# Two parts of packed k in PSUM banks of their own, and idle matmuls between a prologue's TensorE work

## The chip, the cores and the metric

The kernel runs on one core of a Trainium2 chip. The metric is the device time of one execution in microseconds (us), lower being better. An execution is called fast unless it is more than 1.5% above the fastest of its kernel. A profile adds the span (first to last instruction of the core), some 1.7 us less than the device time, and the granted clock of TensorE as a mean over the span.

The profile shows five engines side by side: TensorE (PE, busy for 226.4 us of the 237.5 us span of the kernel before, and PEld for its weight loads, 127.5 us), VectorE (DVE, 115.4 us), ScalarE (ACT, 92.6 us), GpSimd (POOL, 48.4 us) and SyncE (SP), which issues all transfers here but one of 4 KB.

## The reference

A block-wise linear attention with decay, and after it a bilinear feed-forward layer (FFN). Cut to what matters:

```python
batch, n_heads, seq, head_dim = (4, 8, 768, 64)
for b in range(nb):                       # blocks of one sequence
    intra = einsum('bhic,bhjc->bhij', qb, kb) * Dmask
    intra = einsum('bhij,bhjd->bhid', intra, vb)
    inter = einsum('bhid,bhde->bhie', qb * lam_pow, kv_state)
    out[:, :, sl] = intra + inter
    kv_state = lam_block * kv_state + einsum('bhsd,bhse->bhde', kb * rev_pow, vb)
# x: 3072 tokens x 512
return ((x @ w_a) * (x @ w_b)) @ w_out    # 512 -> 1536 -> 512
```

The inputs are float32; the kernel computes in bf16 with float32 sums.

## The kernel before

Tokens are handled as 24 units of 128. The first four units are "packed": their q and k come in as large transfers, two halves of heads each, are scaled on VectorE, transposed on TensorE into PSUM and copied out by ScalarE (`unpack`). Then come score products, a mask on VectorE, state products, outputs into `xT`, and from there the FFN, which fills the rest of the kernel. The work on later units is slipped in between FFN matmuls.

```python
def ps_bank(name, shape, dt, hold=False, ffn=False):   # seven banks in turn
    i = bank["next"]
    ...
    return ps_pool.tile(shape, dt, name=name, tag=f"ps{i}")

def warm(n, cols=128):                                 # idle matmuls on zeros
    for _ in range(n):
        nc.tensor.matmul(idle_ps[:, :cols], lhsT=idle_sb[:, :128], rhs=idle_sb[:, :cols], ...)

def load4(w, i, parts):                                # one half of packed q or k
    ...
    tps = ps_bank("t" + w, [128, 2, PACK, 128], BF16)
    for j in range(2):
        hs = slice(4 * i + 2 * j, 4 * i + 2 * j + 2)
        nc.vector.tensor_mul(...)                      # scale by the decay
        for r in range(PACK):
            nc.tensor.transpose(tps[:, j, r, :], xs4[w][:, r, ...], ident)
        if parts == 2:
            unpack(i, tps, slice(j, j + 1), w)         # ScalarE copies this part out
    if parts == 1:
        unpack(i, tps, slice(0, 2), w)

warm(13, 512)
...
for w, parts in (("q", 1), ("k", 2)):
    for i in range(2):
        load4(w, i, parts)
        if w == "q":
            warm(4)
...
scores4(0)
natural_k((0, 1, 2), (0, 1))
natural_k((0, 1, 2), (2, 3))
scores4(1)
sts = [ps_bank("kv0", ...), ps_bank("kv1", ...), kv_bank()]
for hh in range(2):                                    # state products, by halves
    for u, ps in enumerate(sts):
        for w in range(u + 1):
            kv_mms(ps, w, range(2 * hh, 2 * hh + 2), w == 0)
        if hh:
            kv_copy(u, ps, ("act", "act", "dve")[u])
# ... intra, inter and evac_o of the four units; then the FFN
```

For k, the two parts of a half are copied out one by one, but both lie in one bank: in the profile of before, the transposes of the second part wait for the copy of the first (TensorE idle for 0.67 us in each half, until ScalarE's copy ends).

## Time and profile before

| | device time, us |
|---|---|
| median of 3 runs | 238.28 (237.89 to 238.35) |
| the profiled run | 239.18 (span 237.5, mean clock 0.983) |

The first two lines here are from the page of the profiled run: its span, and the granted clock over 40 equal slices of it, in tenths (9 is 90% or more). The third is from TensorE's timeline: start, length, what, and in brackets how long TensorE was idle before and what ended it.

```profile
span 237.5 us, 4496 instructions
PEclk9959999999999999999999999999999999999998
21.12 1.89 PE L413 MATMUL a_ps<-xT,wa_sb 128*128 128x512 bf16 x7 [0.45 <-ACT xT L352]
```

The slice with a 5 lies in the prologue, where the clock is at half from 10.84 to 17.66 us; in the last slice it falls at 236.09 us, after TensorE's work. The FFN starts at 21.12 us, the moment ScalarE has made its last copy into xT. From there TensorE is nearly solid (busy for 210.37 of the 216.38 us left).

### The profile page before, as it was taken

Reading aid. Unit: us, or ns where it says so; the run is one execution under the profiler, and the core shown is the slowest. Engines: PE = TensorE matmul, PEld = TensorE weight load, DVE = VectorE, ACT = ScalarE, POOL = GpSimd, SP = SyncE. Lnnn points to the kernel's source line nnn. Section 1 sums busy time; section 2 is a strip of 40 time slices with the busy share of each in tenths; the row PEclk is TensorE's granted clock in tenths of the full one; section 3 lists DMA queues with packets and bytes.
Section 4 is the critical chain, followed back from the end, with each engine's and each line's share of the span. In section 5 each row is a group of like instructions: output and inputs, shape, how many; then the busy total and the mean of one; then the engine's idle time right before and its main releaser. Section 6 shows DMA issues by size and latency. Waiting matters only on the chain.

```text
span 237.5 us, 4496 instructions
## 1 busy us (share of the span) xinstructions
PE 226.4 (95%) x1738; PEld 127.5 (54%) x1761; DVE 115.4 (49%) x205; ACT 92.6 (39%) x174; POOL 48.4 (20%) x63
## 2 busy tenths in 40 slices
PE   7599999999999999999999999999999999999993
PEld 2375444458788754454544454544454544444493
DVE  0875756735757646675145575135564214332050
ACT  3548565036554542332143242242341233431161
POOL 6050001234336443203305503003300000000000
PEclk9959999999999999999999999999999999999998
DMA  4999999999979999997929969613120220000311
GB/s 157 297 292 350 348 368 278 284 215 280 228 176 222 191 222 230 222 180 123 212 100 213 185 59 236 150 70 82 27 47 0 88 88 4 0 0 24 111 44 48
DMA packets 94278, 38.32 MB, mean 161 GB/s; under 512 B 81200, under 2 KB 89776, under 8 KB 94256
## 3 DMA queue, kind: packets, MB, share of 16 engines
q1 hardware_dynamic: 94112, 38.02, 70.0%
q8 instruction: 14, 0.23, 0.4%
q14 instruction: 8, 0.07, 0.1%
q10 hardware_dynamic: 144, 0.00, 0.0%
HBM read 28.32 MB, written 6.29 MB: 146 GB/s over the span
## 4 chain that ended last, share of the span: by engine, by line
PE 89%; ACT 3%; DMA 3%; issue 1%; DVE 1%; SPq 0%; DVEq 0%; ACTq 0%
PE a_ps L413 27%; PE b_ps L413 26%; PE op L434 26%; DMA q<-in_q_dram 3%; PE o_ps L345 2%; PE kq L308 2%; PE kvd L359 2%; PE o_ps L335 1%; PE tps L294 1%; ACT scratch L517 1%; ACT xT L352 1%; PE kq L542 1%; ACT o_sb L429 1%; PE tn L526 1%; DVE scratch L503 1%
## 5 line engine op out<-in xcount | busy, mean ns | idle before, releaser
L425 DVE TENSOR_TENSOR ab<-a_sb,b_ps 128x512 bf16<-128x512 bf16 (+2 forms) x96 | 52.6, 553 | 82.7 <-PE b_ps L413 60.2
L413 PE MATMUL a_ps<-xT,wa_sb 128*128 128x512 bf16 (+2 forms) x378 | 76.6, 325 | 1.4 <-ACT xT L352 0.6
L413 PE MATMUL b_ps<-xT,wb_sb 128*128 128x512 bf16 (+2 forms) x379 | 76.7, 325 | 0.2
L420 ACT CAST a_sb<-a_ps 128x512 bf16<-128x512 f32 (+2 forms) x96 | 45.5, 480 | 66.1 <-PE a_ps L413 64.5
L434 PE MATMUL op<-wo_sb,ab 128*128 128x512 bf16 (+2 forms) x300 | 64.3, 362 | 0.9 <-issue 0.5
L413 PEld LDWEIGHTS <-wb_sb 128*128 128x128 bf16 x384 | 34.5, 98 | 28.8 <-issue 0.2
L413 PEld LDWEIGHTS <-wa_sb 128*128 128x128 bf16 x384 | 33.6, 98 | 28.0 <-issue 1.3
L434 PEld LDWEIGHTS <-ab 128*128 128x128 bf16 x312 | 28.7, 98 | 30.1
L320 DVE TENSOR_TENSOR m<-kq,lotri 128x512 bf16<-128x512 f32 x48 | 29.9, 683 | 22.5 <-PE kq L308 20.5
L256 POOL TENSOR_TENSOR qk<-kf,lp_k 128x512 bf16<-128x512 f32 x17 | 17.9, 1051 | 79.9 <-issue 33.5
L429 ACT COPY o_sb<-op 128x512 f32<-128x512 f32 (+2 forms) x26 | 14.2, 553 | 37.2 <-PE op L434 36.7
L261 POOL TENSOR_TENSOR qk<-qf,lp_q 128x512 bf16<-128x512 f32 x20 | 22.0, 1099 | 23.9 <-DMA qf<-in_q_dram 23.9
L352 ACT CAST xT<-o_ps 128x512 bf16<-128x512 f32 x23 | 12.4, 589 | 16.4 <-PE o_ps L345 16.4
L381 DVE TENSOR_TENSOR st<-kvd,bdiag 128x512 bf16<-128x512 f32 x18 | 12.3, 685 | 3.8 <-PE kvd L359 3.8
L296 ACT COPY qkT<-tps 128x1024 bf16<-128x1024 bf16 x7 | 7.1, 1012 | 11.2 <-PE tps L294 11.2
L270 DVE CAST vb<-vf 128x512 bf16<-128x512 f32 x17 | 9.2, 541 | 0.0
L345 PE MATMUL o_ps<-m,vb 128*64 128x128 bf16 x192 | 7.8, 222 | 0.0
L270 POOL CAST vb<-vf 128x512 bf16<-128x512 f32 x7 | 4.4, 630 | 15.6 <-DMA vf<-in_v_dram 15.6
L335 PEld LDWEIGHTS <-st 128*128 128x128 bf16 x80 | 5.4, 98 | 2.8
L308 PE MATMUL kq<-qkT 64*128 64x128 bf16 x160 | 6.6, 218 | 0.0
L345 PEld LDWEIGHTS <-vb 128*64 128x64 bf16 x192 | 5.7, 109 | 1.4
L359 PEld LDWEIGHTS <-qk 128*128 128x128 bf16 x64 | 4.9, 98 | 2.9
(52 smaller groups left out, 87.5 us busy)
## 6 DMA issues: line engine op xcount, KB each, us to landing
vf<-in_v_dram SPq DMA_DIRECT2D x24, 256.0 KB, 5.2
out_dram<-o_sb SPq DMA_DIRECT2D x23, 256.0 KB, 2.3
qf<-in_q_dram SPq DMA_DIRECT2D x20, 256.0 KB, 4.5
kf<-in_k_dram SPq DMA_DIRECT2D x20, 256.0 KB, 4.8
wst<-in_moe_w_a_dram SPq DMA_DIRECT2D x6, 512.0 KB, 9.0
wst<-in_moe_w_b_dram SPq DMA_DIRECT2D x6, 512.0 KB, 8.9
wst<-in_moe_w_out_dram SPq DMA_DIRECT2D x6, 512.0 KB, 8.5
q<-in_q_dram SPq DMA_DIRECT2D x2, 512.0 KB, 5.5
```

Source lines behind the costliest of these rows:

```text
L256: eng_of(eng).tensor_mul(qk[:, 1], raw.pop((u, "k")), lp_k[:, u % NB].to_broadcast([128, H, D]))
L261: eng_of(eng).tensor_mul(U[u]["qk"][:, 0], raw.pop((u, "q")), lp_q[:, u % NB].to_broadcast([128, H, D]))
L270: eng_of(eng).tensor_copy(vb, vf)
L320: nc.vector.tensor_mul(m, kq[i], lotri_bc)
L345: nc.tensor.matmul(d["o"][p, hp, :], lhsT=d["vb"][:, 2 * hp + i, :], rhs=d["m"](i, hp), start=(first and hp == 0), stop=True, skip_group_c ...
L352: nc.scalar.copy(xT[:, :, col:col + BLK], o_ps)
L381: nc.vector.tensor_mul(st[:].rearrange("p hp i d -> p hp (i d)"), ps[:].rearrange("p hp i d -> p hp (i d)"), bdiag_bc)
L413: nc.tensor.matmul(ps[:, :gt], lhsT=w_sb[:, s, f * 128:(f + 1) * 128], rhs=xT[:, s, :gt], start=(s == 0), stop=(s == KS - 1))
L420: nc.scalar.copy(a_sb[:, :gt], ps[:, :gt])
L425: nc.vector.tensor_mul(ab[:, f, :gt], a_sb[:, :gt], ps[:, :gt])
L429: nc.scalar.copy(o_sb[:, lo:hi], op[:, lo:hi])
L434: nc.tensor.matmul(op[:, lo:hi], lhsT=ab[:, f, t * 128:(t + 1) * 128], rhs=wo_sb[:, f, lo:hi], start=(f == 0), stop=(f == FC - 1))
```

## The change

The intent: let the second part of k be transposed without waiting for the first one's copy, and put short idle matmuls where TensorE has gaps so that its clock isn't lowered in the prologue.

```diff
@@ def load4(w, i, parts):
-        tps = ps_bank("t" + w, [128, 2, PACK, 128], BF16)
         for j in range(2):
+            if j == 0 or parts == 2:
+                tps = ps_bank("t" + w, [128, 2, PACK, 128], BF16)
...
             if parts == 2:
                 unpack(i, tps, slice(j, j + 1), w)
+                if i == 0 or j == 0:
+                    warm(3)
@@
     scores4(0)
     natural_k((0, 1, 2), (0, 1))
+    warm(2)
     natural_k((0, 1, 2), (2, 3))
+    warm(2)
     scores4(1)
+    warm(4)
```

## The prediction

> **What bounds the kernel now.** I read the page first, then the chain of waits that ended last, then the timeline of TensorE, of its weight loads and of the other engines over the first 22 us, then stretches of that time with the granted clock. The page says where most of the time is:
>
> ```profile
> PE 226.4 (95%) x1738; PEld 127.5 (54%) x1761; DVE 115.4 (49%) x205; ACT 92.6 (39%) x174; POOL 48.4 (20%) x63
> PE 89%; ACT 3%; DMA 3%; issue 1%; DVE 1%; SPq 0%; DVEq 0%; ACTq 0%
> ```
>
> TensorE is the chain for 89% of the span. The stretches 22 to 60, 60 to 120 and 120 to 237.5 us show it busy for 37.29, 59.36 and 112.89 us. So from the first FFN matmul, at 21.12 us, the rest is a nearly solid stream of about 216 us that the change doesn't touch. All that can move is the time at which that first matmul starts, and that is set by the prologue: the four packed units at 6 to 21 us. There the chain goes from engine to engine:
>
> ```profile
> 9.09 1.57 ACT scratch L517 x2
> 10.70 0.50 PE tk L508 x4
> 11.22 1.15 ACT scratch L517 x2
> 12.41 0.59 PE tk L508 x4
> 13.00 0.97 PE kq L542 x16
> 13.96 1.39 PE tn L526 x12
> 15.36 0.97 PE kq L542 x16
> 16.32 0.75 PE kv L359 x6
> ```
>
> (start, length, what). Two things in it are aimed at. The first is that TensorE's transposes of k (L508) twice wait for ACT's copy (L517) of the previous part, which lies in the same PSUM bank. The weight-load lines show how long the transposes could have been running already:
>
> ```profile
> 10.23 0.10 PEld L508 LDWEIGHTS <-scratch 128*128 128x128 bf16 x1 [0.38 <-DVE scratch L503]
> 10.70 1.04 PE L508 MATMUL tk<-ident,scratch 128*128 128x128 bf16 x8 [0.67 <-ACT scratch L517]
> 11.73 0.10 PEld L508 LDWEIGHTS <-scratch 128*128 128x128 bf16 x1 [0.26 <-DVE scratch L503]
> 12.41 0.59 PE L508 MATMUL tk<-ident,scratch 128*128 128x128 bf16 x4 [0.67 <-ACT scratch L517]
> ```
>
> The weights are in at 10.23 and 11.73 us, the moment VectorE is done, but the matmuls start at 10.70 and 12.41: 0.47 and 0.68 us late. The second is the clock:
>
> ```profile
> 0.60:4.01 3.41, 2.76 (x7) 1.04 (x8) 0.27 (x1) 1.28 (x1) 2.81 (x12) 1.00 0.24 60
> 4.01:7.42 3.41, 2.12 (x14) 0.87 (x13) 1.65 (x4) 0.64 (x3) 0.65 (x2) 1.00 1.05 359
> 7.42:10.84 3.42, 2.02 (x27) 1.43 (x26) 2.94 (x5) 2.57 (x3) 0.00 (x0) 1.00 1.19 306
> 10.84:14.25 3.41, 2.74 (x32) 1.97 (x31) 1.45 (x4) 1.73 (x3) 1.47 (x3) 0.50 1.28 220
> 14.25:17.66 3.41, 3.41 (x41) 3.02 (x39) 3.41 (x7) 1.50 (x2) 2.04 (x4) 0.50 1.08 338
> 232.68:236.09 3.41, 0.90 (x17) 0.72 (x13) 0.00 (x0) 0.53 (x2) 0.00 (x0) 1.00 0.28 82
> ```
>
> (stretch and its length, busy us of PE, PEld, DVE, ACT, POOL, then granted clock, DMA share, GB/s.) The clock is at half from 10.84 to 17.66 us, 6.82 us, and with it nearly all of the prologue's matmuls from the last k transposes to the state products. I cut the stretches at 3.41 us because 6.82 is twice that. The clock column reads 1.00 in the first row, but the idle matmuls' weight loads there are 0.43 us apart and from 4.12 us on five take 0.96 us, so it really was slow until about 4.0 us, which is again such a boundary.
>
> [...] changes at about 4.0, 10.84 and 17.66 us, and again at about 236.1 us, which is 64 windows later. [...] 2.74 us of busy time, mostly transposes and half-array products, didn't free the clock at 14.25 us, while 2.76 us of plain idle matmuls did at 4.0. [...] here I use only starts and ends.
>
> **The change part by part.** It adds no work for VectorE, ScalarE, GpSimd or the queues: their order is the same. TensorE gets 17 idle matmuls of 128 columns: three after each of the first three k parts, then two, two and four. Two more banks go round; as all later banks shift by two of seven, what follows reuses a bank from the same instruction as before, so I expect no new bank wait.
>
> *Separate banks.* The second k part starts at 10.24 in place of 10.70; the third is bound by VectorE and stays at 11.13; the fourth at 11.74 in place of 12.41. The copies are ACT's own queue at 0.57 us each: they start at about 10.06, 10.66, 11.55 and 12.16, in place of 10.06, 11.22, 11.8 and 13.03. By themselves the banks bring the first score product from 12.93 to about 12.3 us: 0.6 us.
>
> *Idle matmuls.* Full-rate cost is taken from the 512-column ones, 0.96 us for nearly five loads, so 0.21 us, or about 0.055 us for 128 columns; at half clock 0.11. The first nine fall in gaps, where TensorE waits for VectorE's 0.61 us beat anyway (four transposes need 0.22), and cost nothing at full clock. The other eight stand in the stream: 8 x 0.055 = 0.44 us at full clock, 0.86 us at half.
>
> *If the clock stays full.* The scores start at 11.74 + 0.26 = 12.0. Before, the first mask came 0.71 us after them; at full clock I estimate 0.45, so VectorE's masks start at 12.45 and, eight in 4.88 us, end at 17.33 (before 18.52). The state products want the fourth mask's bank (14.9) and the last value cast (14.62 + a little), so they start at about 14.95 in place of 16.27 and need some 1.4 us rather than 2.1. ACT's four state copies (1.51 us) then run at about 15.95 to 17.45, in place of 17.97 to 19.48. VectorE's state multiplication ends at 18.0, the last inter product at 18.35, and ACT's three copies into xT (1.57 us) at about 19.1. The first FFN matmul starts at 19.1 to 19.2 in place of 21.12: **2.0 us** gained, of which VectorE's masks and ACT's copies leave no more.
>
> *If the clock falls at the same moment and stays low as long.* The scores start at 12.4 (0.5 earlier), but idle matmuls of 0.86 us at half clock stand before the state products, which then start at about 16.6: **0.3 us lost**.
>
> *If it is low for one window only* (10.84 to 14.25), the scores start at 12.4, the masks end near 18.0, and the first FFN matmul comes at about 19.65: **1.4 us gained**.
>
> *After the prologue.* What is gained reaches the end only if weights and units keep up. DMA is full there (share 1.05 to 1.10) at 350 GB/s: a 512 KB chunk each 1.5 us, two per step of 3.0 us, while TensorE uses two in 3.45 us. Chunk a0 was there at 16.6, so by that estimate a1 is there at 19.6 and b1 at 21.1, and their casts would be wanted at about 19.6 and 21.5. It just fits, and the margin grows by 0.45 us a step.
>
> **The rivals.** (1) *The clock falls anyway.* In the window that ended at 10.84, before, there were 8 plain idle matmuls (about 0.45 us of streaming) and 19 transposes. After, 14 plain ones: 0.77 us, 22%. The last window of the kernel had 17 plain matmuls, 0.90 us busy, and the clock fell after it. If transposes count for nothing, 22% isn't enough and the clock falls at 10.84; if they count fully, 33 matmuls of 128 columns are as many columns as in the window from 4.01 (about 4,100), after which it held. And the added idle work may yet free it at 14.25. Time: 238.6 if low throughout, 236.9 if for one window. (2) *The banks alone work and the idle matmuls eat it*: time as before, 238.2; the 0.86 us above against 0.6 speaks for it. (3) *DMA takes over in the first FFN steps*: a new wait at the casts of a1 and b1 of up to about 0.5 us; time 236.8 with the clock full. Against it: VectorE and ACT show no wait for weights there now. (4) [...] where they fall may differ from run to run; the three runs of before lie within 0.46 us, so I don't expect much from that.
>
> **Range and chances.** I give 45% to a full clock (238.28 - 2.0, with some 0.2 lost to rivals: about 236.4), 30% to one low window (236.9 to 237.4) and 25% to a clock that falls as before (238.2 to 238.6). The weighted mean is 0.45 x 236.4 + 0.30 x 237.1 + 0.25 x 238.4 = 237.1; I say 237.0, as the middle case is the median. Eight in ten: 236.1 to 238.5. A gain of 2% is 4.77 us, over twice the most that the prologue gives, and no path I see costs so much either: faster 0.01, same 0.98, slower 0.01.
>
> **What would show it right or wrong.** In the changed profile: no wait of the k transposes for ACT, and starts at about 10.24 and 11.74 us; granted clock 1.00 from 7 us to the end of the prologue (or half for one stretch of 3.41 us); first mask at about 12.5 rather than 13.64; first FFN matmul at 19.1 to 19.7 rather than 21.12; a span shorter by just that difference. I am wrong if the clock is full and the first FFN matmul still starts after 20.5 us (then a wait I didn't see bounds the prologue), if it starts early and the span is not shorter by as much (DMA), or if the clock is at half for 6.8 us again.

Where a cut is marked, words of the text are taken out. No term of the forecast's sum is among them: it was 0.45 x 236.4 + 0.30 x 237.1 + 0.25 x 238.4 = 237.1 us, put as 237.0. A "window", there and below, is a stretch of 3.41 us: half of the 6.82 us at half clock. "Where they fall" in the fourth rival speaks of the windows' places. That transposes might do less for the clock than plain matmuls wasn't shown: all that the trace had on it were the two windows named, with 2.74 and 2.76 us of busy time.

## The result, and the profile after

| | runs | median, us | range, us |
|---|---|---|---|
| before | 4 | 238.26 | 237.89 to 238.35 |
| after | 4 | 237.51 | 237.14 to 237.77 |

The ratio is 0.997, with a 95% interval from 0.9953 to 0.9987. (A ratio is the mean time of one kernel's fast runs over that of the other's of the same rounds, so not quite the ratio of the medians.) The gain is real and small, 0.75 us by the medians.

The two profiles differ by more: 2.1 us of span. The same lines of the page after the change:

```profile
span 235.4 us, 4530 instructions
PE 225.1 (96%) x1755; PEld 126.2 (54%) x1778; DVE 115.7 (49%) x205; ACT 92.9 (39%) x174; POOL 49.4 (21%) x63
PEclk9999999999999999999999999999999999999999
PE 85%; DMA 6%; DVE 2%; ACT 2%; issue 2%; SPq 1%; DVEq 0%; ACTq 0%
```

The clock is full in every slice. TensorE has 17 matmuls more on record than before and is busy for 1.3 us less. The k transposes (now L509) and the first FFN matmul, from TensorE's timeline:

```profile
10.18 0.40 PE L509 MATMUL tk<-ident,scratch 128*128 128x128 bf16 x4
10.41 0.33 PE L194 MATMUL idle<-idle_sb 128*128 128x128 bf16 x3
11.08 0.40 PE L509 MATMUL tk<-ident,scratch 128*128 128x128 bf16 x4 [0.34 <-DVE scratch L504]
11.32 0.33 PE L194 MATMUL idle<-idle_sb 128*128 128x128 bf16 x3
11.69 0.40 PE L509 MATMUL tk<-ident,scratch 128*128 128x128 bf16 x4
...
19.35 1.89 PE L413 MATMUL a_ps<-xT,wa_sb 128*128 128x512 bf16 x7 [0.46 <-ACT xT L352]
```

Both waits for ScalarE (10.70 and 12.41 us in the prediction's lines of before) are gone. The second part starts at 10.18 us rather than 10.70, the fourth at 11.69 rather than 12.41, and the FFN at 19.35 rather than 21.12 us: 1.77 us earlier. From there to the last group of output matmuls (229.28 us after, 230.76 before) it takes 209.93 us, against 209.64: 0.29 us of the gain are given back. Two waits of TensorE in its timeline are longer than before (0.27 us for the first) or new; the last two lines are VectorE's and GpSimd's just before the first of them:

```profile
57.46 0.38 PE L413 MATMUL a_ps<-xT,wa_sb 128*128 128x128 bf16 x4 [0.63 <-DVE ab L425]
...
101.60 0.40 PE L308 MATMUL kq<-qkT 64*128 64x128 bf16 x8 [0.30 <-DMA qkT<-qk]
...
56.17 1.04 DVE L256 TENSOR_TENSOR qk<-kf,lp_k 128x512 bf16<-128x512 f32 x1
55.62 1.04 POOL L256 TENSOR_TENSOR qk<-kf,lp_k 128x512 bf16<-128x512 f32 x1 [1.40 <-DMA kf<-in_k_dram]
```

The first wait belongs to the price of an early start. VectorE scales one unit's k there (L256) and then makes the `ab` that TensorE waits for. In the profile of before that took 0.69 us, from 57.94 us, after GpSimd had ended its own work at 57.54; here it took 1.04 us and began while GpSimd was at the same kind of work. Over all 14 profiles VectorE's operation takes 0.68 to 1.43 us, and TensorE's wait goes with it, from 0.27 to about 1.0 us. In the ten profiles in which it takes longer than 0.7 us, it began 0.2 to 0.9 us before GpSimd's running operation ended, and the longer that was, the longer it took; in the other four there was at most 0.1 us of this. The stretch from the FFN's start to the last group takes 209.60 to 209.64 us in the three profiles whose FFN starts after 20 us, and 209.61 to 210.47 in the other eleven; in the changed kernel's second profile it is 210.29. So 0 to 0.9 us of a prologue's gain is given back at about 57 us, and not the same in each execution. That the overlap with GpSimd is the cause is read from these traces; no run tested it.

The remaining 0.6 us between the spans lie after TensorE's last work: from the start of that last group to the end of the span it is 6.1 us after and 6.7 before. This isn't the change's: 11 of the 14 profiles, the old bank layout's among them, have 6.1 to 6.2 us there, and three have 6.5 to 6.7. One profile therefore tells the time only to about half a microsecond.

The chain of waits, in order of time (start, length, what), shows what the prologue hangs on now:

```profile
11.69 0.40 PE tk L509 x4
12.09 0.38 PE kq L545 x8
...
12.52 1.90 DVE m L320 x3
...
14.84 0.33 PE idle L194 x4
15.17 0.48 PE kv L359 x6
...
16.19 0.18 ACT st L379
...
17.73 1.57 ACT xT L352 x3
```

Where TensorE's own work at half clock stood (scores, transposes back, scores), there are now VectorE's masks (L320), and after them ScalarE's state copies (L379) and copies into xT (L352).

The question for the experiments is then: why is the change worth 1.8 us between two prologues and 0.75 us between timed runs, and which part of it does what?

### The profile page after: what moved, and what is told of

Its sections match the earlier page's. It is cut to its first block, busy times and chain, and to the rows that moved or that the text cites. A ratio compares the mean times of both kernels' runs of the same rounds, so it can differ in the third digit from the quotient of the medians.

```text
span 235.4 us, 4530 instructions
## 1 busy us (share of the span) xinstructions
PE 225.1 (96%) x1755; PEld 126.2 (54%) x1778; DVE 115.7 (49%) x205; ACT 92.9 (39%) x174; POOL 49.4 (21%) x63
## 4 chain that ended last, share of the span: by engine, by line
PE 85%; DMA 6%; DVE 2%; ACT 2%; issue 2%; SPq 1%; DVEq 0%; ACTq 0%
PE op L434 26%; PE a_ps L413 25%; PE b_ps L413 24%; DMA k<-in_k_dram 3%; DMA qkT<-qk 3%; PE o_ps L345 2%; PE kq L308 2%; DVE m L320 2%; PE kvd L359 2%; PE o_ps L335 1%; PE tps L294 1%; ACT xT L352 1%; ACT o_sb L429 1%; SPq L206 1%; ACT st L379 1%
## 5 line engine op out<-in xcount | busy, mean ns | idle before, releaser
L320 DVE TENSOR_TENSOR m<-kq,lotri 128x512 bf16<-128x512 f32 x48 | 29.9, 683 | 20.5 <-PE kq L308 19.6
L256 POOL TENSOR_TENSOR qk<-kf,lp_k 128x512 bf16<-128x512 f32 x17 | 17.9, 1053 | 76.9 <-issue 31.4
L261 POOL TENSOR_TENSOR qk<-qf,lp_q 128x512 bf16<-128x512 f32 x20 | 23.1, 1154 | 23.8 <-DMA qf<-in_q_dram 23.8
L352 ACT CAST xT<-o_ps 128x512 bf16<-128x512 f32 x23 | 12.4, 590 | 16.9 <-PE o_ps L345 16.9
L270 DVE CAST vb<-vf 128x512 bf16<-128x512 f32 x17 | 8.4, 496 | 0.0
L194 PE MATMUL idle<-idle_sb 128*128 128x128 bf16 (+1 forms) x38 | 7.2, 322 | 1.3 <-DVE idle_sb L189 1.3
```

Of the source, the lines that this page charges most:

```text
L256: eng_of(eng).tensor_mul(qk[:, 1], raw.pop((u, "k")), lp_k[:, u % NB].to_broadcast([128, H, D]))
L261: eng_of(eng).tensor_mul(U[u]["qk"][:, 0], raw.pop((u, "q")), lp_q[:, u % NB].to_broadcast([128, H, D]))
L270: eng_of(eng).tensor_copy(vb, vf)
L320: nc.vector.tensor_mul(m, kq[i], lotri_bc)
L352: nc.scalar.copy(xT[:, :, col:col + BLK], o_ps)
```

## The experiments

**Theory A.** In the profile of before the clock changes at 4.01, 10.84, 17.66 and 236.09 us. These lie 6.83, 6.82 and 218.43 us apart, which is 2, 2 and 64 windows of 3.41 us to within 0.2 us. (Two later profiles, of the banks alone and of the later eight alone, each have the clock at half for a single window, from 11.72 to 15.13 and from 11.88 to 15.29 us.) The windows' place differs from execution to execution: by the spacing of the first idle matmuls' weight loads, 0.43 us and then 0.21, the clock is first freed at 4.36 and at 5.43 us in two profiles of the changed kernel. The theory, then, is that in some executions of the kernel before the clock is at half for two windows of the prologue, in others for one or none. The profiled run was one of the costly ones; the timed runs were mostly not. The banks bring their part in any case, the idle matmuls only where the clock would have fallen. **Rivals:** B, the profiled run was slow for another reason; C, the idle matmuls carry all of it; D, they carry nothing and only cost.

The twelve runs were in three groups of four. Each has six timed executions, and each group shares eleven of the kernel before. Each group ran on another chip, so medians are best compared within a group. The first four runs below are the first group, the cold starts and the idle transposes the second, the later eight alone and the last three kernels the third.

### The changed kernel again, and the clocks of the kernel before

No edit.

> The changed kernel again, for the runs of both kernels side by side. Theory A ([...] the profiled run of the kernel before had the clock at half for two windows, 6.8 us, and its timed runs for one window or none, so that the timed gain of 0.75 us is less than the 2.1 us between the two profiles): runs of the kernel before show granted clocks that differ from run to run, between about 0.985 and 1.000, and their spans are the longer the lower the clock; the changed kernel shows 1.000 throughout; ratio about 0.997. Theory B (the profiled run of before was slow for another reason, such as DMA): the clock of before is about 0.983 in all its runs and doesn't go with the span; ratio 0.997 too.

Measured: 237.46 us (236.82 to 239.86), before 238.40 (237.88 to 239.62); ratio 0.9968, interval 0.9931 to 1.0004. Every execution comes with its mean clock. One window at half takes 0.5 x 3.41 / 237 = 0.007 off the mean, two take 0.014, and a fall after the last matmul another 0.003 (in the profile of before) or somewhat more. The 33 runs of the kernel before, from all three groups, sort by that:

| mean clock | which is | runs | mean time, us | range, us |
|---|---|---|---|---|
| 0.983 to 0.986 | two windows at half | 7 | 239.45 | 238.84 to 240.12 |
| 0.989 to 0.993 | one window | 18 | 238.48 | 237.88 to 239.23 |
| 0.996 to 0.999 | none in the prologue, by this sum | 8 | 238.22 | 237.97 to 238.45 |

So Theory A holds and B falls: clock and time go together (239.45, 238.48 and 238.22 us), the profiled run of before was of the first row, and its first three timed runs, whose clocks aren't on record, lie within the range of the other two. Two windows go with about 1.2 us, one with about 0.3; the order is the same in each of the three groups (1.0 to 1.4 us and 0.1 to 0.4). The rows overlap, so the clock isn't all that differs between runs. Which windows were low is worked out from the mean alone: the only profile of this kernel is of the first row. The changed kernel read 0.997 to 1.000 in nine of its ten runs (the four above and these six), with a mean of 237.41 us, and 0.986 once, with 239.86 (at 1.3% above the fastest). So "1.000 throughout" was too much to expect: the change makes a low clock rarer, and doesn't rule it out. Between runs without a low clock, 238.22 and 237.41, there are 0.8 us. The mean clock doesn't explain them, but it can miss low time before the record of the clock begins (the cold starts below read 0.990 to 1.000), and the runs are of several groups; the idle matmuls alone, below, are the cleaner comparison.

### Separate banks alone

```diff
-                if i == 0 or j == 0:
-                    warm(3)
...
-    warm(2)   # twice
-    warm(4)
```
(taken from the changed kernel; the banks stay)

> Separate banks alone, no added idle matmuls. Theory A (banks and clock both matter): k transposes start at about 10.2 and 11.7 us with no wait for ScalarE; the clock falls in some runs (mean clock under 1.000 in at least two of six); 237.6 to 237.9 us, that is half to all of the gain in the runs where the clock stays up. Theory C (the idle matmuls carry all of the gain): no faster than the kernel before, 238.2 us.

Measured: 237.53 us (236.91 to 238.43), ratio 0.9962 (0.9933 to 0.9992). In the profile k's second and fourth parts start at 10.10 and 11.60 us, with no wait for ScalarE. The clock was 0.993 in three of six runs. The profiled run was one of those; here are two windows of it (stretch, its length, busy us of PE, PEld, DVE, ACT and POOL with counts, granted clock, DMA share, GB/s) and the start of the FFN:

```profile
8.31:11.72 3.41, 1.94 (x23) 1.25 (x23) 2.74 (x5) 2.72 (x5) 0.24 (x1) 1.00 1.26 267
11.72:15.13 3.41, 3.41 (x46) 2.82 (x46) 2.34 (x4) 2.12 (x4) 1.74 (x4) 0.50 1.23 243
...
19.61 1.89 PE L413 MATMUL a_ps<-xT,wa_sb 128*128 128x512 bf16 x7 [0.45 <-ACT xT L352]
```

With one window at half the FFN still starts at 19.61 us, 0.26 us after that of the changed kernel. Theory C falls: the banks alone reach about the same median as the whole change (237.46 in this group). What the idle matmuls add to the banks in time isn't shown: the means of six are 237.64 us for the banks alone and 237.78 for the whole change, with its one run of low clock.

### Idle matmuls alone

```diff
+        tps = ps_bank("t" + w, [128, 2, PACK, 128], BF16)
         for j in range(2):
-            if j == 0 or parts == 2:
-                tps = ps_bank("t" + w, [128, 2, PACK, 128], BF16)
```
(taken from the changed kernel; all 17 added idle matmuls stay)

> All 17 added idle matmuls, k's two parts in one bank as before. Theory A: clock 1.000 in all runs, first FFN matmul 0.3 to 0.7 us later than in the changed kernel (about 19.8 us), 237.7 to 238.0 us. Theory C (the banks carry nothing): as the changed kernel, 237.5 us. Theory D (the idle matmuls carry nothing and cost 0.4 us): 238.5 us or more.

Measured: 237.97 us (237.74 to 238.25), ratio 0.9977 (0.9956 to 0.9999), clock 1.000 in all six. The waits for the bank are there as before, and the FFN starts at 19.89 us:

```profile
10.70 0.38 PE L508 MATMUL tk<-ident,scratch 128*128 128x128 bf16 x4 [0.51 <-ACT scratch L519]
...
12.25 0.38 PE L508 MATMUL tk<-ident,scratch 128*128 128x128 bf16 x4 [0.55 <-ACT scratch L519]
...
19.89 1.89 PE L413 MATMUL a_ps<-xT,wa_sb 128*128 128x512 bf16 x7 [0.45 <-ACT xT L352]
```

Against the changed kernel, whose clock is as full, the separate banks are thus worth 19.89 - 19.35 = 0.54 us, of which 0.05 were there already at the first k transposes (9.63 and 9.58 us). In time it is 237.97 - 237.46 = 0.51 us, in one group and with a high clock in all runs but one. Against the profile of before, with the same banks and two windows at half, the clock is worth 21.12 - 19.89 = 1.23 us, which agrees with the 1.2 us of the table. D falls too, if narrowly: this kernel is faster than before, by 0.4 us in the medians, with an interval that just leaves out 1. Its runs lie closest together among those of its group.

### Which idle matmuls matter: the nine between k's transposes

```diff
     natural_k((0, 1, 2), (0, 1))
-    warm(2)
     natural_k((0, 1, 2), (2, 3))
-    warm(2)
     scores4(1)
-    warm(4)
```

> Separate banks and only the nine idle matmuls between k's transposes; none of the eight that stand later in the stream. Theory A, in which the window with the k transposes decides: clock 1.000 in all runs and 0.1 to 0.3 us faster than the changed kernel, as 0.44 us of idle work is out of the stream: 237.2 to 237.4 us. If the later eight are needed to hold the clock: clock under 1.000 in some runs and 237.6 us or more.

Measured: 237.52 us (237.08 to 237.95), ratio 0.9958 (0.9935 to 0.9980), clock 0.998 to 1.000 in all six. The FFN starts at 19.29 us. With the nine alone the clock held, but taking out the other eight gained nothing like 0.1 to 0.3 us: the last four of these had stood where TensorE waits for VectorE's masks anyway (without them it is idle for 0.31 us there, and the state products start at 15.09 us, with them at 15.15).

### The later eight alone

```diff
-                if i == 0 or j == 0:
-                    warm(3)
```

> Separate banks and only the later eight idle matmuls (two, two and four), none between the k transposes. If these don't help the clock, as they come after the window that decides: clocks as with banks alone (0.993 in about half of the runs) and, in those, eight idle matmuls at half clock in the stream: 237.6 to 238.2 us, no faster than banks alone.

Measured: 237.47 us (237.16 to 239.22), ratio 0.9958 (0.9926 to 0.9990); the clock was 0.993 in three of six, as with the banks alone. In the profiled run, one of those three, the FFN starts at 20.02 us, 0.41 after that of the banks alone with one window at half (0.07 of it were there already at k's second part, 10.17 against 10.10 us):

```profile
8.47:11.88 3.41, 2.02 (x24) 1.34 (x24) 2.65 (x5) 2.71 (x5) 0.33 (x1) 1.00 1.27 263
...
20.02 1.24 PE L413 MATMUL a_ps<-xT,wa_sb 128*128 128x512 bf16 x5 [0.45 <-ACT xT L352]
```

The later eight come after that window (the first at 13.63 us, with the clock at half since 11.88). They don't hold the clock (0.993 in three of six), and where it has fallen they cost, 0.34 to 0.41 us at the FFN's start. The median doesn't show the cost (it lies below the 237.6 us expected), the prologue does.

### A prologue that starts at half clock: before, banks, all

The 13 idle matmuls at the very start, after which the clock was free at 4.0 to 6.1 us, are taken out of three kernels:

```diff
-    warm(13, 512)
     new_xT(0)
```

> The kernel before without its 13 idle matmuls at the start, so that the clock starts the prologue at half and nothing in it is dense enough to free it until the state products. Theory A (a prologue at half clock is what the slow runs of before show): first FFN matmul at 21.0 to 22.0 us, 239.2 to 239.8 us, runs closer together than those of the kernel before, since the window's place hardly matters. If the clock isn't a cost: 238.3 us.

> The same start at half clock with the separate banks alone. Theory A: the banks' waits of about 0.5 and 0.7 us go at half clock too: 0.5 to 0.8 us faster than the cold kernel before (238.6 to 239.0 us). If the banks pay only where the clock is full: as the cold kernel before.

> The same start at half clock with the whole change. Prediction's case of a clock that stays low: the eight later idle matmuls (0.86 us at half clock) eat the banks' gain: within 0.3 us of the cold kernel before, and 0.6 us or more slower than the cold one with banks alone. Rival: the nine idle matmuls between the k transposes free the clock a window earlier than in the cold kernel before (matmul spacing changes from about 0.107 to 0.055 us before 15 us): then faster than the cold one with banks alone.

| start at half clock | median, us | ratio to before | clock freed at, us | FFN starts at, us |
|---|---|---|---|---|
| before | 238.69 | 1.0004 (0.9972 to 1.0037) | 17.7 | 21.25 |
| banks alone | 237.69 | 0.9962 (0.9934 to 0.9991) | 15.8 | 19.89 |
| whole change | 237.28 | 0.9940 (0.9910 to 0.9971) | 11.5 | 19.42 |

(The last two columns are from the profiled runs. The time at which the clock is freed is where the trace's clock record begins; the clock column shows 1.00 before that too, but the matmuls' spacing, about 0.11 us before and 0.055 us after, shows the half clock.) In the cold kernel before, the windows that end at 10.87 and 14.28 us were busy for 2.75 and 2.66 us and the clock stayed at half; after the one that ends at 17.70 us, busy for all its 3.42 us and with the first state products in it, it was free. The cold kernel before lies 0.5 us under the least time expected, although its FFN starts as late as in the profile of before (whose span is 0.5 us longer only by its end, after TensorE's last work). So a prologue at half clock took less time here than the runs with two low windows in the table, 239.45 us; why stays open. The banks gain 1.0 us here, more than at full clock and more than the 0.5 to 0.8 expected; but the windows of these two profiles also lie differently, so how much of that is the banks' own isn't settled. For the whole change the profile shows the rival right, and the prediction's case of a low clock that stays wrong (in time the 0.4 us between the two changed kernels are within their intervals): with the nine idle matmuls TensorE was busy all through a window, and the clock was free at 11.5 us, 4 us before it was with the banks alone, whose windows lay otherwise:

```profile
8.12:11.53 3.41, 3.41 (x33) 2.95 (x31) 2.92 (x5) 2.90 (x4) 0.00 (x0) 1.00 1.24 278
```

### Idle transposes in place of the idle matmuls

```diff
-                    warm(3)
+                    idle_transposes(3)      # nc.tensor.transpose of the same zeros, 128 x 128
...
-    warm(2) / warm(2) / warm(4)
+    idle_transposes(2) / idle_transposes(2) / idle_transposes(4)
```

> The changed kernel with its 17 added idle matmuls turned into idle transposes of the same size. If transposes count for nothing [...]: clocks as with banks alone (under 0.997 in about half of the runs) and 237.6 to 238.2 us. If they count like matmuls: clock 0.997 to 1.000 in nearly all runs and 237.5 us as the changed kernel.

Measured: 237.51 us (236.94 to 237.78), ratio 0.9953 (0.9926 to 0.9980); clock 1.000 in all six. Its window with k's transposes:

```profile
8.70:12.11 3.41, 2.66 (x35) 1.87 (x37) 2.58 (x4) 2.71 (x4) 0.51 (x1) 1.00 1.29 253
```

That window has four plain idle matmuls and the beginning of the scores; all else in it is transposes, and the clock held, where with the banks alone, with as many plain ones, it fell (8.31 to 11.72 us, busy for 1.94 us against 2.66 here). So here the clock held with idle transposes as it did with plain idle matmuls (0.997 to 1.000 in nine of the changed kernel's ten runs). By the runs alone, six of six against three of six in another group, this could still be chance.

### More idle work in the gaps, and ScalarE's chain

The guess was that fuller gaps hold the clock more surely. This kernel has the banks, 9 idle matmuls after each half of q rather than 4, then 6, 10 and 6 in place of 3, 3 and 3, and no later ones.

```diff
-                    warm(3)
+                    warm((6, 10, 6)[2 * i + j])
...
-                warm(4)
+                warm(9)
```

> Separate banks, the gaps between the packed transposes filled with idle matmuls (9 after each q half, then 6, 10 and 6 after the first three k parts), none of the later eight. Theory A: clock held in all runs, first FFN matmul at about 19.3 us as with nine, 237.1 to 237.5 us, and no run over 238.3. If the idle work gets in the way of the transposes: first FFN matmul after 19.5 us.

Measured: 237.26 us (237.03 to 237.58), ratio 0.9940 (0.9914 to 0.9966), clock 0.999 to 1.000 in all six, FFN at 19.44 us in the profiled run. It has no run with a low clock, and its median is the lowest among the kernels that keep the first 13 idle matmuls, if within noise: the changed kernel wasn't in the same group, and the intervals overlap. That the fuller gaps hold the clock more surely than the nine alone (0.998 to 1.000) isn't shown.

The next thing on the path is then ScalarE: four state copies, then three copies into xT. Two kernels bring the state copies forward by ordering the state products by unit, one with the filled gaps and one with the nine.

```diff
-    for hh in range(2):
-        for u, ps in enumerate(sts):
+    for u, ps in enumerate(sts):
+        for hh in range(2):
             ...
-            if hh:
-                kv_copy(u, ps, ("act", "act", "dve")[u])
+        kv_copy(u, ps, ("act", "act", "dve")[u])
```

> As the run with the gaps filled, and the state products in the order of units (both halves of a unit together), so that ScalarE's state copies needn't wait for all three units. If ScalarE's chain of four state copies and three copies into xT sets the first FFN matmul: copies start at about 15.6 in place of 16.2 us and the first FFN matmul comes 0.2 to 0.4 us earlier (about 19.0 us), the rest then being bound by VectorE's masks; 236.9 to 237.2 us. If the weights' transfers set it: no change.

> Separate banks, only the nine idle matmuls between the k transposes, and the state products in the order of units: first FFN matmul at about 19.0 us, 236.9 to 237.3 us; clock as with the nine alone (0.998 to 1.000 in nearly all runs).

Measured: 237.32 (237.22 to 237.60) and 237.36 us (237.27 to 238.02), ratios 0.9942 and 0.9947; FFN at 19.45 and 19.39 us. Expected were about 19.0: a miss. ScalarE's timeline of the first, and two lines of TensorE's, say why:

```profile
15.74 1.51 ACT L379 CAST st<-kv 64x256 bf16<-64x256 f32 x4 [1.01 <-POOL vb L270]
17.27 1.07 ACT L352 CAST xT<-o_ps 128x512 bf16<-128x512 f32 x2
18.81 0.58 ACT L352 CAST xT<-o_ps 128x512 bf16<-128x512 f32 x1 [0.46 <-PE o_ps L335]
...
15.26 0.83 PE L359 MATMUL kv<-vb,scratch 128*128 128x128 bf16 x12 [0.31 <-DVE m L320]
...
18.16 0.62 PE L335 MATMUL o_ps<-scratch,st 128*128 128x128 bf16 x8
```

The state copies do start 0.55 us earlier than with the filled gaps alone (16.29), and two xT copies with them. But the last one waits 0.46 us for TensorE's output of the fourth unit. TensorE shows no wait from 15.26 us on, when VectorE's fourth mask lets the state products begin, up to that output, and it comes to it no sooner than with the gaps alone (18.16 against 18.15 us). VectorE's own state operation, behind its eight masks, ends at 18.10 us, just before that group. So chains of about the same length end there, and shortening ScalarE's gives nothing.

## Why the prediction was right or wrong

It said 237.0 us, in 236.1 to 238.5, with 0.98 for "within 2%". Measured were 237.51 and, in the second group of runs, 237.46. The range and the class were right; the gain was predicted at 1.3 us and measured at 0.75 to 0.94. There is luck in it: the case that came true, the full clock, was put at about 236.4 us, and 237.51 lies 1.1 above that. The stated 237.0 came near because cases that didn't come true were averaged in.

- **The FFN's start sets the time.** Right in the main. In both profiles TensorE is nearly solid from there (busy for 210.37 of 216.38 us before, 210.10 of 216.05 after). Of the 1.77 us that the prologue gained, 0.29 are lost on the way in this profile and 0.65 in the changed kernel's second one (210.29 us), chiefly in the wait at 57 us, which was not expected as such; 0.2 had been allowed for rivals in the full-clock case.
- **The banks remove two waits.** Right in place and size: starts at 10.24 and 11.74 were said, 10.18 and 11.69 measured. The 0.6 us by themselves came out as 0.54 at the FFN's start with a full clock and as 0.51 in time against the idle matmuls alone, and as about 0.8 between timed runs whose mean clock was high. The latter compares runs of several groups, so it is the weakest of the three.
- **The prologue at full clock.** Right within 0.25 us all along: scores at 12.0 said and 12.02 measured, first mask 12.45 and 12.52, end of the masks 17.33 and 17.40, state products 14.95 and 15.15, state copies 15.95 and 16.19, FFN 19.1 to 19.2 and 19.35. The last three carry the 0.33 us of the four idle matmuls ahead of the state products on the chain, but without these (the nine alone) the FFN's start is 19.29, so they cost next to nothing.
- **The step that was mis-sized** is the sum's base: "238.28 - 2.0". The 2.0 us are the distance from an execution with two windows at half clock, which the profile of before happened to be (239.18 us), and were taken off a median of executions that mostly had one such window or none. From two windows to none is 1.2 us, from one to none 0.3. Taken off the mean of the runs with two windows, the sum gives 239.45 - 2.0 = 237.45 us, beside 237.41 measured without a low clock. That the windows may lie differently from run to run, as these runs show (first freed at 4.01, 4.36 and 5.43 us in three profiles), was its fourth rival, and it set that aside: "the three runs of before lie within 0.46 us, so I don't expect much from that". Three runs were too few; over 33 the range is 237.88 to 240.12. That the profiled run lay 0.9 us above all three was the sign that was not read.
- **A clock that falls at the same moment and stays low, 0.3 us lost.** Not seen as described in a profile. What was seen of its parts: the later eight at half clock cost 0.34 to 0.41 us at the FFN's start (20.02 against 19.61), where 0.86 in the stream was said; and in the one low run of the changed kernel, 239.86, the time is that of the runs of before with two windows at half, or worse. Which of its windows were low isn't known, as that run left no profile.
- **One low window, FFN at about 19.65.** Seen at 19.61, though in the kernel with the banks alone.
- **Rival 1, the clock falls anyway because transposes count for nothing.** Wrong: the clock was 0.997 to 1.000 in nine of the changed kernel's ten runs, and with idle transposes in place of the idle matmuls it was 1.000 in six of six. (The prediction says that it uses only starts and ends of matmuls; the shares of this rival, such as its 22%, are busy times.)
- **Rival 2, idle work eats the banks' gain.** Wrong at full clock (237.51 us against 238.26 before).
- **Rival 3, the weights arrive too late.** A wait came, as said, and cost TensorE nothing there: VectorE waited 0.81 us for the second chunk of w_a, and the second block of FFN matmuls still started 3.67 us after the first, as before.

## What to carry to other kernels

A profile is one execution. Where the granted clock differs between executions, as here (0.983 to 0.999 over 33 runs of the kernel before), compare the profile's time with the timed runs before taking a gain off their median, and sort the runs by their clock. The two waits for a bank (0.67 us each in the profile of before) are gone in all eleven profiles with the banks of their own. The idle matmuls were insurance, worth at most what the bad windows cost times how often they came: about 1.2 us in 7 of the 33 runs and 0.3 in 18. Here the nine between k's transposes held the clock (0.998 to 1.000 in six of six), the later eight didn't (0.993 in three of six). With the banks in place no gain in time from them is shown. When two engines' chains end at the same place, shortening one may give nothing, as here (FFN at 19.45 us against 19.44). And a gain at the start has to be followed to the end: here 0.29 us of 1.77 went into later waits.

## What these traces show of the clock, and what they leave open

- With 17 idle transposes the clock was 1.000 in six of six executions, with the banks alone 0.993 in three of six, and the window with nine of the transposes (8.70 to 12.11 us) held although all but 0.46 us of its 2.66 us of busy time was in transposes.
- The clock fell after windows that were busy for 2.02 us (before), 1.94 (banks alone) and 2.02 us (later eight alone) of 3.41, and held after windows with 2.12 (before, from 4.01 us) and 2.19 us (idle matmuls alone). The gap between 2.02 and 2.12 us is small, and a trace can lack some matmul records (the page of before has 384 weight loads of `wa_sb` and 378 matmuls on it), so no line is drawn from it.
- What frees the clock again is not settled by busy time: 2.76 us of plain 512-column matmuls did (before, until 4.01 us), 3.13 us of transposes and a few plain and half-array products didn't (cold start with banks alone, 8.99 to 12.41 us), and 3.41 us did in which 20 of 33 matmuls were transposes (cold start with the whole change, 8.12 to 11.53 us).
- The clock record starts only with the first change: at 4.01 us in the profile of before, and the three kernels that began at half clock show 1.00 in their first stretches and means of 0.990 to 1.000.
